# Cross network, last layer: the first half of the batch by features, the second half by rows

## The chip, the cores and the metric

The kernel runs on one NeuronCore of a Trainium2 chip. What is measured is the device time of one execution, in microseconds (us). A core has TensorE (PE: matrix multiplication into PSUM), VectorE (DVE: elementwise work), ScalarE (ACT: here it moves results out of PSUM and adds a bias), GpSimd (POOL: a few copies) and SyncE (SP: it issues DMAs, in order). The DMAs themselves are carried out by 16 DMA engines that the queues share. On-chip tiles lie in SBUF, which has 128 partitions.

## The reference

```python
B, F, D, L = 4096, 26, 16, 6          # Din = 416
def reference(x0, ws, bs):            # x0 (4096, 416), ws (6, 416, 416), bs (6, 416), all bf16
    x = x0
    for l in range(ws.shape[0]):
        x = x0 * (x @ ws[l] + bs[l]) + x
    return x
```

Six layers; each multiplies the batch by a 416 x 416 matrix, adds a bias, multiplies by the input and adds the layer's own input.

## The kernel before, in words

The 416 features are three blocks of 128 (`NK`, main) and a remainder of 32 (`R`). The batch of 4096 is two halves of 2048 (`s`), each of four groups of 512 columns (`g`).

*Layers 0 to 4 go by features.* The activations are transposed: `XM[i]` holds features on partitions (three blocks) and the batch along the row, `XR[i]` the remainder's 32 features, the four groups stacked on partitions. For a half `s` and a block `m`, `mm_full` (lines 201 to 207) gives 12 matmuls of 128x512 for each group, each of 32 output columns, so that four run side by side; `mm_row` (209) adds the remainder's part; `mm_rem` (215) computes the remainder's outputs. Results lie in PSUM, which is handed out two banks at a time, four such pairs in turn (`two_banks`, 142). `ew_main` (172) then takes 1024 columns: ScalarE moves them to a tile `t` with the bias (line 169), VectorE multiplies by x0 (line 179) and adds the layer's input (line 180). `ew_rem` (191) does the same for the remainder, 512 columns. Of `t` there are six buffers.

*The last layer (l = 5) goes by rows.* Its output has to lie in DRAM with the batch along rows. Therefore activations are the stationary operand there: a quad `q` (eight of them, four for each half) is 4 x 128 rows of the batch; each 128 rows by 416 outputs take three matmuls (`mm_q_full`, line 357) and one for the remainder (366) and one for the bias (371). ScalarE copies the result out of PSUM (383), VectorE multiplies by `X0rows` (384) and adds `XLrows` (385), SP stores rows of 832 B (387, 389). The last two quads do this for 128 rows at a time (`ew_single`, lines 396 to 401), with the sum put off until the next product has been issued.

For that, the last layer needs x0 and its own input by rows. `X0rows` is loaded from DRAM by eight DMAs (128). `XLrows` comes from layer 4: as soon as a half and block is done there, a transposing DMA (`xl_dmat`, line 229) turns it from SBUF to SBUF; the remainder's 32 features go through a transposing DMA into `scrR` (299) and a copy on POOL (300).

*What sets the order.* The schedule is manual: each engine does its instructions in the order in which the program writes them, and waits on semaphores where an operand isn't there. SP issues all stores and transposes of this stage in one order on one hardware queue (`q1`).

Of the kernel before, what the change touches and what calls it, by code (L numbers as in the profile page):

```python
# [10 lines left out]
ALU = mybir.AluOpType  # L11
BF16 = mybir.dt.bfloat16
# [4 lines left out]
def kernel(  # L17
# [7 lines left out]
    nc = tc.nc  # L25
    B, D = x0.shape
    L = ws.shape[0]
    P = 128
    NK = 3
    R = D - NK * P  # L30
    assert R == 32 and B == 4096 and D == 416 and L >= 2
    NS = 2
    NG = 4
    CW = 512
    SW = NG * CW
    NBT = B // P
# [20 lines left out]
    bT = const.tile([R, D // R, R], BF16)  # L57
    bM = const.tile([P, NK, L], FP32)
    bR = const.tile([P, L], FP32)
    X0rows = big.tile([P, NBT, D], BF16)  # L60
    XLrows = big.tile([P, NBT, D], BF16)
    scrR = [big.tile([P, 4, P], BF16, name=f"scrR{s}") for s in range(NS)]
    xrt = [big.tile([P, 16, R], BF16, name=f"xrt{s}") for s in range(NS)]
    xrem = [big.tile([P, 16, R], BF16, name=f"xrem{s}") for s in range(NS)]
# [4 lines left out]
    def col0(s, g):  # L69
        return SW * s + CW * g  # L70
# [54 lines left out]
        load_wr(nc.sync, g, 1, L)  # L125
    for l in range(2, L):
        load_wm(nc.sync, l)
    for q in range(8):
        nc.sync.dma_start(X0rows[:, 4 * q:4 * q + 4, :], x0_v[:, 4 * q:4 * q + 4, :])

    def fill_wd(l0, l1):
        for g in range(NG):
# [9 lines left out]
    def two_banks():  # L142
        n = turn[0]
        i = first_order[n] if n < len(first_order) else (2, 1, 3, 0)[(n - len(first_order)) % 4]
        turn[0] += 1
        return PS[:, 2 * i:2 * i + 2, :]
# [25 lines left out]
    def ew_main(l, s, m, h, pt, cur, nxt):  # L172
        c0 = col0(s, 2 * h)
        t = ew_copy(l, m, pt)
        x0c = XM[0][:, m, c0:c0 + 2 * CW]
        if l == 0:
            nc.vector.tensor_tensor(out=nxt[:, m, c0:c0 + 2 * CW], in0=t, in1=x0c, op=ALU.mult)  # L177
            return
        nc.vector.tensor_tensor(out=t, in0=t, in1=x0c, op=ALU.mult)  # L179
        nc.vector.tensor_tensor(out=nxt[:, m, c0:c0 + 2 * CW], in0=t, in1=cur[:, m, c0:c0 + 2 * CW], op=ALU.add)  # L180
# [20 lines left out]
    def mm_full(l, s, m, g, pts, cur, first, last):  # L201
        c0 = col0(s, g)
        for k in range(NK):
            for q in range(4):
                nc.tensor.matmul(pts[g // 2][32 * q:32 * q + 32, g % 2, :], lhsT=WM[:, l, k, 128 * m + 32 * q:128 * m + 32 * q + 32],  # L205
                                 rhs=cur[:, k, c0:c0 + CW], start=(first and k == 0), stop=(last and k == NK - 1),
                                 tile_position=(0, 32 * q), skip_group_check=True)
# [17 lines left out]
    def new_pts():  # L225
        return [two_banks() for h in range(2)]

    def xl_dmat(s, k, nxt):
        nc.sync.dma_start_transpose(out=XLrows[:, 16 * s:16 * s + 16, 128 * k:128 * k + 128],
                                    in_=nxt[:, k, SW * s:SW * s + SW])  # L230

# [58 lines left out]
    def rem_pair(l, cur, curR, nxtR, feeds_last):  # L292
        pr2 = two_banks()
        for s in range(NS):
            mm_rem(l, s, pr2[:, s, :], cur, curR)
        for s in range(NS):
            ew_rem(l, s, pr2[:, s, :], curR, nxtR)
            if feeds_last:
                nc.sync.dma_start_transpose(out=scrR[s][:], in_=nxtR[:, CW * s:CW * s + CW])
                nc.gpsimd.tensor_copy(XLrows[:, 16 * s:16 * s + 16, NK * P:D].rearrange("p (g i) r -> p i g r", g=NG),  # L300
                                      scrR[s][:].rearrange("p i (g r) -> p i g r", g=NG))

    def rem_first(pb):
        pr2 = two_banks()
# [10 lines left out]
    for l in range(1, LL):  # L315
        nxt, nxtR = XM[1 + (l % 2)], XR[1 + (l % 2)]
        feeds_last = (l == LL - 1)
        tiles = [(s, m) for s in range(NS) for m in range(NK)]
        pts = {}

        def finish(t):
            s, m = t
            for h in range(2):
                ew_main(l, s, m, h, pts[t][h], cur, nxt)
            if feeds_last:
                xl_dmat(s, m, nxt)

        for n in range(0, len(tiles), 2):
            ta, tb = tiles[n], tiles[n + 1]
            pts[ta] = new_pts()  # L330
            for g in range(NG):
                mm_full(l, ta[0], ta[1], g, pts[ta], cur, True, False)
            mm_row(l, ta[0], ta[1], pts[ta], curR, False, True)
            pts[tb] = new_pts()
            mm_row(l, tb[0], tb[1], pts[tb], curR, True, False)
            finish(ta)
            for g in range(NG):
                mm_full(l, tb[0], tb[1], g, pts[tb], cur, False, True)
            finish(tb)
            if n == 0:  # L340
                rem_pair(l, cur, curR, nxtR, feeds_last)
        cur, curR = nxt, nxtR

    l = LL
    quads = [(s, i) for s in range(NS) for i in range(4)]
    NQ = len(quads)
    KD = NK * P

    def q_cols(q, g):
        s, i = quads[q]  # L350
        c = col0(s, g) + 128 * i
        return slice(c, c + 128)

    def mm_q_full(q, py, gs, first):
        for g in gs:
            for k in range(NK):
                nc.tensor.matmul(py[g // 2][:, g % 2, 0:D], lhsT=cur[:, k, q_cols(q, g)], rhs=WM[:, l, k, :],  # L357
                                 start=(first and k == 0), stop=((not first) and k == NK - 1), skip_group_check=True)
# [2 lines left out]

    def mm_q_rows(qs, pys, begun):
        for q, py in zip(qs, pys):
            s, i = quads[q]
            for g in range(NG):
                nc.tensor.matmul(py[g // 2][:, g % 2, 0:D], lhsT=curR[32 * g:32 * g + 32, CW * s + 128 * i:CW * s + 128 * i + 128],
                                 rhs=WR[32 * g:32 * g + 32, l, :], start=not (q == begun and g < 2), stop=False,
                                 tile_position=(32 * g, 0), skip_group_check=True)
        for q, py in zip(qs, pys):
            for g in range(NG):  # L370
                nc.tensor.matmul(py[g // 2][:, g % 2, 0:D], lhsT=pick[1][32 * g:32 * g + 32, :],
                                 rhs=bsb[32 * g:32 * g + 32, :], start=False, stop=(q == begun and g < 2), tile_position=(32 * g, 0),
                                 skip_group_check=True)

    o4 = [big.tile([P, NG, D], BF16, name=f"o4_{q}") for q in range(3)]

    def ew_pair(q, h, py):
        s, i = quads[q]
        b0 = 16 * s + 8 * h + i
        t = tpool.tile([P, 2 * CW], BF16, name="t")  # L380
        tv = t[:, 0:2 * D].rearrange("p (a d) -> p a d", a=2)
        o = o4[q][:, 2 * h:2 * h + 2, :] if q < 3 else opool.tile([P, 2, D], BF16, name="o")[:]
        nc.scalar.copy(tv, py[h][:, :, 0:D])  # L383
        nc.vector.tensor_tensor(out=tv, in0=tv, in1=X0rows[:, b0:b0 + 5:4, :], op=ALU.mult)  # L384
        nc.vector.tensor_tensor(out=o, in0=tv, in1=XLrows[:, b0:b0 + 5:4, :], op=ALU.add)  # L385
        if q >= 3:
            nc.sync.dma_start(out_v[:, b0:b0 + 5:4, :], o)
        elif h == 1:
            nc.sync.dma_start(out_v[:, b0 - 8:b0 + 5:4, :], o4[q][:])

    def ew_single(q, g, py):
        s, i = quads[q]
        b = 16 * s + 4 * g + i
        t = tpool.tile([P, 2 * CW], BF16, name="t")
        o = opool.tile([P, 2, D], BF16, name="o")
        nc.scalar.copy(t[:, 0:D], py[g // 2][:, g % 2, 0:D])  # L396
        nc.vector.tensor_tensor(out=t[:, 0:D], in0=t[:, 0:D], in1=X0rows[:, b, :], op=ALU.mult)  # L397

        def close():
            nc.vector.tensor_tensor(out=o[:, 0, :], in0=t[:, 0:D], in1=XLrows[:, b, :], op=ALU.add)  # L400
            nc.sync.dma_start(out_v[:, b, :], o[:, 0, :])

        return close

    for q in range(0, NQ - 2, 2):
        py = [new_pts()]
        mm_q_full(q, py[0], (0, 1), True)
        py.append(new_pts())
        mm_q_rows((q, q + 1), py, q)
        ew_pair(q, 0, py[0])  # L410
        mm_q_full(q, py[0], (2, 3), False)
        ew_pair(q, 1, py[0])
        for h in range(2):
            mm_q_full(q + 1, py[1], (2 * h, 2 * h + 1), False)
            ew_pair(q + 1, h, py[1])
    pending = []
    for q in range(NQ - 2, NQ):
        py = new_pts()
        mm_q_rows((q,), (py,), None)
        for g in range(NG):  # L420
            mm_q_full(q, py, (g,), False)
            pending.append(ew_single(q, g, py))
            keep = 0 if (q, g) in ((NQ - 2, NG - 1), (NQ - 1, 0), (NQ - 1, NG - 1)) else 1
            while len(pending) > keep:
                pending.pop(0)()


# [28 lines left out]
```

## Time and profile before

| | |
|---|---|
| median of 3 timed runs | 130.84 us (130.61 to 131.32) |
| the profiled execution | 130.19 us, its span 128.13 us |
| granted TensorE clock | 1.00 |
| PE busy / VectorE busy / ScalarE busy | 122.7 / 105.2 / 83.5 us |
| layer 5 on PE | from 102.79 to 123.77 us |
| layer 5 on VectorE | from 106.94 to 125.39 us |
| landing of the last store | 127.3 us |

A line of a group or of the order of time names engine, line, operation, `out<-in`, and partitions x elements; `x6` is a count. "PE busy" counts matmuls in flight, so 96% doesn't say that PE is at its peak. An issue on SP is written SPq; "DMA to landing" is the time from the issue to the last write's confirmation. In a DMA view a queue's line has packets, MB, and the packets' time as a share of 16 engines; a share over 100% means that packets overlap.

### The profile page before, as it was taken

To read this page: it belongs to the slowest core of one execution; us is meant where nothing else is said; L and a number is where in the kernel's file an instruction comes from. 1 tells how busy PE (TensorE), PEld (TensorE's weight loads), DVE (VectorE), ACT (ScalarE), POOL (GpSimd) and SP (SyncE) were. 2 spreads that over 40 slices of the span, in tenths; PEclk is the share of its full clock that TensorE was granted. 3 is DMA by queue.
4 is the path that set the end of the run, shared out by engine and by line. 5 is a ranking of instruction groups with operands and counts; after the bars stand their busy time and mean duration, and the time that the engine had idled before them with its cause. 6 is when DMAs were issued, how large, how long until landed. Compare 5 with 4: busy or idle time off the path is not lost. (4 is left out here: it accounts for less than half of the span.)

```text
span 128.1 us, 3929 instructions
## 1 busy us (share of the span) xinstructions
PE 122.7 (96%) x1677; PEld 54.7 (43%) x1677; DVE 105.2 (82%) x192; ACT 83.5 (65%) x94; POOL 8.6 (7%) x29
## 2 busy tenths in 40 slices
PE   6999999999999999999999999999999999999960
PEld 3344344444444444444444544444444445445420
DVE  3347959357979898989898989898989999999991
ACT  2117559489666849666849666749666777567860
POOL 4282000120000000000000000000000300000000
PEclk9999999999999999999999999999999999999999
DMA  3999999999990000000000000000398899986663
GB/s 91 259 157 192 207 187 263 229 329 332 336 314 24 5 0 8 0 0 5 0 5 0 5 0 5 0 0 5 69 140 177 167 122 246 192 283 216 210 225 103
DMA packets 42029, 16.36 MB, mean 128 GB/s; under 512 B 30838, under 2 KB 42012, under 8 KB 42012
## 3 DMA queue, kind: packets, MB, share of 16 engines
q1 hardware_dynamic: 40512, 15.70, 55.0%
q10 hardware_dynamic: 1500, 0.42, 1.6%
q8 instruction: 13, 0.21, 0.7%
q14 instruction: 4, 0.03, 0.1%
HBM read 6.15 MB, written 3.41 MB: 75 GB/s over the span
## 5 line engine op out<-in xcount | busy, mean ns | idle before, releaser
L169 ACT ACTIVATE t<-PS,bM 128x1024 bf16<-128x1024 f32 x56 | 58.1, 1115 | 21.2 <-PE PS L211 21.2
L205 PE MATMUL PS<-XM,WM 128*32 128x512 bf16 x1152 | 65.2, 379 | 0.0
L205 PEld LDWEIGHTS <-WM 128*32 128x32 bf16 x1152 | 29.8, 97 | 33.7 <-issue 5.1
L179 DVE TENSOR_TENSOR t<-t,XM 128x1024 bf16<-128x1024 bf16 x48 | 33.4, 695 | 4.1 <-ACT t L169 4.1
L180 DVE TENSOR_TENSOR XM<-t,XM 128x1024 bf16<-128x1024 bf16 x48 | 33.5, 699 | 3.1
L357 PE MATMUL PS<-WM,XM 128*128 128x416 bf16 x96 | 17.9, 340 | 0.0
L240 PE MATMUL PS<-XM,WM 128*128 128x512 bf16 x72 | 16.5, 383 | 0.1
L383 ACT CAST t<-PS 128x832 bf16<-128x832 f32 x12 | 10.2, 852 | 5.0 <-PE PS L357 2.5
L357 PEld LDWEIGHTS <-XM 128*128 128x128 bf16 x96 | 8.9, 98 | 8.7 <-issue 2.1
L240 PEld LDWEIGHTS <-WM 128*128 128x128 bf16 x72 | 6.9, 99 | 9.4 <-issue 2.1
L222 PE MATMUL PS<-XM,WM 128*32 128x512 bf16 x120 | 8.2, 379 | 0.0
L193 ACT ACTIVATE t<-PS,bR 128x512 bf16<-128x512 f32 x10 | 6.8, 694 | 1.9 <-POOL WD L133 1.9
L385 DVE TENSOR_TENSOR o<-t,XLrows 128x832 bf16<-128x832 bf16 x12 | 7.1, 592 | 0.5
L211 PE MATMUL PS<-XR,WR 32*128 32x512 bf16 x96 | 7.3, 379 | 0.0
L384 DVE TENSOR_TENSOR t<-t,X0rows 128x832 bf16<-128x832 bf16 x12 | 7.0, 586 | 0.0
L300 POOL COPY XLrows<-scrR 128x512 bf16<-128x512 bf16 x2 | 1.4, 698 | 72.7 <-DMA scrR<-XR 72.7
L177 DVE TENSOR_TENSOR XM<-t,XM 128x1024 bf16<-128x1024 bf16 x7 | 4.7, 690 | 1.5 <-ACT t L169 1.4
L150 PE MATMUL PS<-warm 128*128 128x512 bf16 (+2 forms) x13 | 4.6, 536 | 1.0 <-DVE warm L87 1.0
L186 ACT ACTIVATE t<-PS,bM 128x512 bf16<-128x512 f32 x4 | 2.6, 685 | 3.8 <-PE PS L247 3.8
L162 ACT COPY XR<-xrt 64x256 bf16<-64x256 bf16 x2 | 1.2, 621 | 5.7 <-DVE xrt L161 5.7
L161 DVE STREAM_TRANSPOSE xrt<-xrem 64x256 bf16<-64x256 bf16 (+1 forms) x5 | 2.2, 477 | 3.2 <-DMA xrem<-in_x_dram 3.2
L396 ACT CAST t<-PS 128x416 bf16<-128x416 f32 x8 | 4.0, 506 | 1.0 <-PE PS L357 0.8
(44 smaller groups left out, 54.4 us busy)
## 6 DMA issues: line engine op xcount, KB each, us to landing
X0rows<-in_x_dram SPq DMA_DIRECT2D x8, 416.0 KB, 7.5
WM<-in_ws_dram SPq DMA_DIRECT2D x5, 312.0 KB, 6.7
out_dram<-o SPq DMA_DIRECT2D x3, 416.0 KB, 3.2
out_dram<-o SPq DMA_DIRECT2D x6, 208.0 KB, 2.5
out_dram<-o SPq DMA_DIRECT2D x8, 104.0 KB, 1.7
WR<-in_ws_dram SPq DMA_DIRECT2D x4, 130.0 KB, 5.7
WM<-in_ws_dram ACTq DMA_DIRECT2D x1, 312.0 KB, 3.4
XM<-in_x_dram SPq DMA_TRANSPOSE x8, 4.8
```

The source lines that it names most:

```text
L169: nc.scalar.activation(t[:], pt.rearrange("p a b -> p (a b)"), ACT.Identity, bias=bM[:, m, l:l + 1], scale=1.0)
L179: nc.vector.tensor_tensor(out=t, in0=t, in1=x0c, op=ALU.mult)
L180: nc.vector.tensor_tensor(out=nxt[:, m, c0:c0 + 2 * CW], in0=t, in1=cur[:, m, c0:c0 + 2 * CW], op=ALU.add)
L193: nc.scalar.activation(tr[:, 0:CW], pr, ACT.Identity, bias=bR[:, l:l + 1], scale=1.0)
L205: nc.tensor.matmul(pts[g // 2][32 * q:32 * q + 32, g % 2, :], lhsT=WM[:, l, k, 128 * m + 32 * q:128 * m + 32 * q + 32], rhs=cur[:, k, c0:c ...
L211: nc.tensor.matmul(pts[g // 2][:, g % 2, :], lhsT=WR[32 * g:32 * g + 32, l, 128 * m:128 * m + 128], rhs=curR[32 * g:32 * g + 32, CW * s:CW ...
L222: nc.tensor.matmul(pr[32 * g:32 * g + 32, :], lhsT=WM[:, l, k, NK * P:D], rhs=cur[:, k, c0:c0 + CW], start=False, stop=(k == NK - 1), tile ...
L240: nc.tensor.matmul(pt[:, gl, :], lhsT=WM[:, 0, k, 128 * m:128 * m + 128], rhs=cur[:, k, c0:c0 + CW], start=(first and k == 0), stop=(last ...
L357: nc.tensor.matmul(py[g // 2][:, g % 2, 0:D], lhsT=cur[:, k, q_cols(q, g)], rhs=WM[:, l, k, :], start=(first and k == 0), stop=((not first ...
L383: nc.scalar.copy(tv, py[h][:, :, 0:D])
L384: nc.vector.tensor_tensor(out=tv, in0=tv, in1=X0rows[:, b0:b0 + 5:4, :], op=ALU.mult)
L385: nc.vector.tensor_tensor(out=o, in0=tv, in1=XLrows[:, b0:b0 + 5:4, :], op=ALU.add)
```

## The change

The last layer does its two halves in two ways. The first half (s = 0) goes by features as the layers before it: `full_first` and `row_first` for the matmuls, `ew_main` and `ew_rem` for the rest, into `XM` and `XR`. Its result goes to rows by transposing DMAs into a new tile `Orows` (`to_rows`, and `rem_to_rows` for the remainder through `scrR` and POOL), and from there to DRAM by three stores of 128, 128 and 160 columns (`store_first`: 2048 pieces of 256, 256 and 320 B). So the first half needs neither `X0rows` nor `XLrows`: these tiles are halved, `X0rows` is loaded by one DMA, and layer 4's three transposes and the remainder's for the first half go. The second half stays by rows, as four quads: quad 0 in pairs of 128-row groups, quad 1's first two as a pair, the other ten alone. The order of VectorE's products (step 0) and sums (step 1) of these eleven units is written out in `order`. The output tiles `o4` go; all row stores use `o`, of which there are ten buffers. `mm_q_rows` now issues a quad's remainder and bias matmuls together.

```diff
+    HB = NBT // NS
+    X0rows = big.tile([P, HB, D], BF16)
+    XLrows = big.tile([P, HB, D], BF16)
+    Orows = big.tile([P, HB, D], BF16)
...
-    for q in range(8):
-        nc.sync.dma_start(X0rows[:, 4 * q:4 * q + 4, :], x0_v[:, 4 * q:4 * q + 4, :])
+    nc.sync.dma_start(X0rows[:], x0_v[:, HB:NBT])
...
+    def to_rows(rows, s, k, x):
+        nc.sync.dma_start_transpose(out=rows[:, :, 128 * k:128 * k + 128], in_=x[:, k, SW * s:SW * s + SW])
+
+    def rem_to_rows(rows, s, xR):
+        nc.sync.dma_start_transpose(out=scrR[s][:], in_=xR[:, CW * s:CW * s + CW])
+        nc.gpsimd.tensor_copy(rows[:, :, NK * P:D].rearrange("p (g i) r -> p i g r", g=NG),
+                              scrR[s][:].rearrange("p i (g r) -> p i g r", g=NG))
...
+        if feeds_last:
+            rem_to_rows(XLrows, 1, nxtR)
...
-            if feeds_last:
-                xl_dmat(s, m, nxt)
+            if feeds_last and s == 1:
+                to_rows(XLrows, 1, m, nxt)
...
+    def ew_rows(q, g0, g1, py):
+        b, n = 4 * g0 + q, g1 - g0
+        t = tpool.tile([P, 2 * CW], BF16, name="t")
+        tv = t[:, 0:n * D].rearrange("p (a d) -> p a d", a=n)
         o = opool.tile([P, 2, D], BF16, name="o")
+        nc.scalar.copy(tv, py[g0 // 2][:, g0 % 2:g0 % 2 + n, 0:D])
+
+        def product():
+            nc.vector.tensor_tensor(out=tv, in0=tv, in1=X0rows[:, b:b + 4 * n - 3:4, :], op=ALU.mult)
+
+        def total():
+            nc.vector.tensor_tensor(out=o[:, 0:n, :], in0=tv, in1=XLrows[:, b:b + 4 * n - 3:4, :], op=ALU.add)
+            nc.sync.dma_start(out_v[:, HB + b:HB + b + 4 * n - 3:4, :], o[:, 0:n, :])
+
+        return product, total
+
+    def store_first(d0, d1):
+        nc.sync.dma_start(out_v[:, 0:HB, d0:d1], Orows[:, :, d0:d1])
...
+    opened = [[False] * NG for m in range(NK)]
+    pt0 = new_pts()
+    full_first(0, pt0, 0)
+    row_first(0, pt0, (0, 1))
+    pt1 = new_pts()
+    row_first(1, pt1, ())
+    ew_main(l, 0, 0, 0, pt0[0], cur, nxt)
+    full_first(0, pt0, 1)
+    to_rows(Orows, 0, 0, nxt)
+    store_first(0, P)
+    for h in range(2):
+        full_first(1, pt1, h)
+    to_rows(Orows, 0, 1, nxt)
+    pr = two_banks()
+    mm_rem(l, 0, pr[:, 0, :], cur, curR)
+    ew_rem(l, 0, pr[:, 0, :], curR, nxtR)
+    rem_to_rows(Orows, 0, nxtR)
+    store_first(P, 2 * P)
+    pt2 = new_pts()
+    full_first(2, pt2, 0)
+    row_first(2, pt2, (0, 1))
+    py = [new_pts()]
+    mm_q_rows((0,), py, None)
+    ew_main(l, 0, 2, 0, pt2[0], cur, nxt)
+    full_first(2, pt2, 1)
+    to_rows(Orows, 0, 2, nxt)
+    for h in range(2):
+        mm_q_full(0, py[0], (2 * h, 2 * h + 1), False)
+        for step in ew_rows(0, 2 * h, 2 * h + 2, py[0]):
+            step()
...
+    order = [(0, 0), (1, 0), (0, 1), (1, 1), (2, 0), (3, 0), (2, 1), (3, 1), (4, 0), (5, 0), (4, 1), (6, 0), (5, 1), (6, 1),
+             (7, 0), (8, 0), (7, 1), (9, 0), (8, 1), (10, 0), (9, 1), (10, 1)]
+    units = []
+
+    def evict(q, g0, g1, pyq):
+        units.append(ew_rows(q, g0, g1, pyq))
+        while order and order[0][0] < len(units):
+            u, step = order.pop(0)
+            units[u][step]()
+            if (u, step) == (3, 1):
+                store_first(2 * P, D)
```

More of the change, by code (lines that the diff above doesn't have):

```diff
@@ L59 @@
     bR = const.tile([P, L], FP32)
-    X0rows = big.tile([P, NBT, D], BF16)
-    XLrows = big.tile([P, NBT, D], BF16)
+    HB = NBT // NS
+    X0rows = big.tile([P, HB, D], BF16)
+    XLrows = big.tile([P, HB, D], BF16)
+    Orows = big.tile([P, HB, D], BF16)
     scrR = [big.tile([P, 4, P], BF16, name=f"scrR{s}") for s in range(NS)]
@@ L226, in new_pts @@
         return [two_banks() for h in range(2)]
-    def xl_dmat(s, k, nxt):
-        nc.sync.dma_start_transpose(out=XLrows[:, 16 * s:16 * s + 16, 128 * k:128 * k + 128],
-                                    in_=nxt[:, k, SW * s:SW * s + SW])
+    def to_rows(rows, s, k, x):
[4 more added lines that the diff above has]
+                              scrR[s][:].rearrange("p i (g r) -> p i g r", g=NG))
     def first_layer(s):
@@ L297, in rem_pair @@
             ew_rem(l, s, pr2[:, s, :], curR, nxtR)
-            if feeds_last:
-                nc.sync.dma_start_transpose(out=scrR[s][:], in_=nxtR[:, CW * s:CW * s + CW])
-                nc.gpsimd.tensor_copy(XLrows[:, 16 * s:16 * s + 16, NK * P:D].rearrange("p (g i) r -> p i g r", g=NG),
-                                      scrR[s][:].rearrange("p i (g r) -> p i g r", g=NG))
+        if feeds_last:
+            rem_to_rows(XLrows, 1, nxtR)
     def rem_first(pb):
@@ L324, in finish @@
                 ew_main(l, s, m, h, pts[t][h], cur, nxt)
-            if feeds_last:
-                xl_dmat(s, m, nxt)
+            if feeds_last and s == 1:
+                to_rows(XLrows, 1, m, nxt)
         for n in range(0, len(tiles), 2):
@@ L344 @@
     l = LL
-    quads = [(s, i) for s in range(NS) for i in range(4)]
-    NQ = len(quads)
+    nxt, nxtR = XM[1 + (l % 2)], XR[1 + (l % 2)]
+    NQ = 4
     KD = NK * P
     def q_cols(q, g):
-        s, i = quads[q]
-        c = col0(s, g) + 128 * i
+        c = col0(1, g) + 128 * q
         return slice(c, c + 128)
@@ L363, in mm_q_rows @@
         for q, py in zip(qs, pys):
-            s, i = quads[q]
             for g in range(NG):
-                nc.tensor.matmul(py[g // 2][:, g % 2, 0:D], lhsT=curR[32 * g:32 * g + 32, CW * s + 128 * i:CW * s + 128 * i + 128],
+                nc.tensor.matmul(py[g // 2][:, g % 2, 0:D], lhsT=curR[32 * g:32 * g + 32, CW + 128 * q:CW + 128 * q + 128],
                                  rhs=WR[32 * g:32 * g + 32, l, :], start=not (q == begun and g < 2), stop=False,
                                  tile_position=(32 * g, 0), skip_group_check=True)
-        for q, py in zip(qs, pys):
             for g in range(NG):
@@ L373, in mm_q_rows @@
                                  skip_group_check=True)
[L375 to L379, printed above, removed]
+    def ew_rows(q, g0, g1, py):
+        b, n = 4 * g0 + q, g1 - g0
         t = tpool.tile([P, 2 * CW], BF16, name="t")
[L381 to L394, printed above, removed]
-        o = opool.tile([P, 2, D], BF16, name="o")
[L396 to L419, printed above, removed]
-        for g in range(NG):
[L421 to L425, printed above, removed]
+        tv = t[:, 0:n * D].rearrange("p (a d) -> p a d", a=n)
@@ new lines, in full_first, with row_first @@
+    def full_first(m, pt, h):
+        for g in (2 * h, 2 * h + 1):
+            mm_full(l, 0, m, g, pt, cur, not opened[m][g], opened[m][g])
+        if opened[m][2 * h]:
+            ew_main(l, 0, m, h, pt[h], cur, nxt)
+    def row_first(m, pt, begun):
+        for g in range(NG):
+            nc.tensor.matmul(pt[g // 2][:, g % 2, :], lhsT=WR[32 * g:32 * g + 32, l, 128 * m:128 * m + 128],
+                             rhs=curR[32 * g:32 * g + 32, 0:CW], start=(g not in begun), stop=(g in begun),
+                             tile_position=(32 * g, 0), skip_group_check=True)
+            opened[m][g] = True
@@ new lines @@
+    units = []
[6 more added lines that the diff above has]
+                store_first(2 * P, D)
+    py = [new_pts()]
+    mm_q_full(1, py[0], (0, 1), True)
+    py.append(new_pts())
+    mm_q_rows((1, 2), py, 1)
+    evict(1, 0, 2, py[0])
+    for q in (1, 2, 3):
+        if q == 3:
+            py.append(new_pts())
+            mm_q_rows((3,), (py[2],), None)
+        for g in range(2 if q == 1 else 0, NG):
+            mm_q_full(q, py[q - 1], (g,), False)
+            evict(q, g, g + 1, py[q - 1])
```

## The prediction

> **What bounds the kernel now.** I read the page first (busy shares, the span in slices, the chain that ended last), then the last stage in order of time, engine by engine, and then what the DMA queue and SP do there.
>
> The page, shares of the span, the span in 40 slices and the chain:
>
> ```profile
> PE 122.7 (96%) x1677; PEld 54.7 (43%) x1677; DVE 105.2 (82%) x192; ACT 83.5 (65%) x94; POOL 8.6 (7%) x29
> ...
> DVE  3347959357979898989898989898989999999991
> ...
> DMA  3999999999990000000000000000398899986663
> ...
> DVE 6%; issue 0%; DVEq 0%
> ```
>
> VectorE (DVE) is at 9 in the last ten slices, and the chain that ended last is VectorE alone. DMA is idle in the middle and works again only from slice 29 on. The last stage of VectorE in order of time (start, length):
>
> ```profile
> 99.35 1.10 DVE L179 TENSOR_TENSOR t<-t,XM 128x1024 bf16<-128x1024 bf16 x1
> 100.55 1.01 DVE L180 TENSOR_TENSOR XM<-t,XM 128x1024 bf16<-128x1024 bf16 x1
> 101.49 0.68 DVE L179 TENSOR_TENSOR t<-t,XM 128x1024 bf16<-128x1024 bf16 x1
> ...
> 106.33 0.69 DVE L180 TENSOR_TENSOR XM<-t,XM 128x1024 bf16<-128x1024 bf16 x1
> 106.94 0.58 DVE L384 TENSOR_TENSOR t<-t,X0rows 128x832 bf16<-128x832 bf16 x1
> 107.61 0.59 DVE L385 TENSOR_TENSOR o<-t,XLrows 128x832 bf16<-128x832 bf16 x1
> 108.12 0.58 DVE L384 TENSOR_TENSOR t<-t,X0rows 128x832 bf16<-128x832 bf16 x1
> ```
>
> VectorE enters the last layer at 106.94, while PE began it at 102.79. It then runs a product and a sum every 1.13 us until it has caught up with PE near the end: PE's last group starts at 121.49 and takes 2.28 (123.77), the last sum ends at 125.39, its store lands at 127.3. So both engines end together; neither alone can give much. Now SP and the DMAs, from the DMA view of a stretch of transposes, the source view of the transposes' line, and SP in order of time:
>
> ```profile
> q1 hardware_dynamic: 3080, 0.78, 125.2%
> ...
> XLrows<-XM SPq DMA_TRANSPOSE x2, 5.1
> ```
>
> ```profile
> L229 SPq DMA_TRANSPOSE XLrows<-XM x6: 1929/2722/3287, 90.6 to 107.4; - x6
> ...
> DMA to landing us min/median/max: 4.7/5.5/6.2
> ```
>
> ```profile
> 90.64 5.82 SPq L229 DMA_TRANSPOSE XLrows<-XM  x2
> 96.56 2.53 SPq L299 DMA_TRANSPOSE scrR<-XR  x2
> 99.18 11.33 SPq L229 DMA_TRANSPOSE XLrows<-XM  x4
> 110.60 3.64 SPq L389 DMA_DIRECT2D out_dram<-o  x3
> ```
>
> One transposing DMA of 128x2048 occupies SP for 1.9 to 3.3 us and lands 4.7 to 6.2 us after its issue. Today SP only issues: what it waits for is VectorE, never a landing, and the first store starts when the last transpose has been issued (110.60). The 3080 packets of 256 B in the first DMA view filled 125.2% of 3 us on 16 engines: 19.5 ns each.
>
> **The change part by part.** The profiled execution took 130.19 us, 2.06 more than its span of 128.13; its last store landed 0.85 before the span's end. The median of the timed runs is 130.84, 0.65 above it. I sum against the profiled execution and add the 0.65 at the end.
>
> *PE.* New: the first half's 144 column-split matmuls (six blocks of 24; 96 of them took 94.25 to 99.55, so 1.33 a block), 7.95; their row matmuls, 8 in 0.54 (99.55 to 100.09) and 4 in 0.27; the remainder's 16, 0.86 (89.29 to 90.15); four quads at 2.21 (118.81 to 121.02) and their row matmuls 0.47 + 0.81 + 0.47. Sum 20.2 against 102.79 to 123.77 = 21.0: 0.8 less. It does not reach the end, since VectorE is later.
>
> *VectorE.* In layer 4 one of POOL's two copies goes; the sums beside them took 1.10 and 1.01 instead of 0.69, some 0.37 a copy, and the layer before has an idle 0.29 at this place. VectorE therefore starts the last layer about 0.36 earlier, at 106.6. There: six pairs by features at 1.36 (four took 101.49 to 106.94), 8.2; remainder 0.87; the moved copy 0.37; quad 0's two pairs 2.26; then the fixed order, which puts no sum right behind its own product: 1.02 for the pair of 832 (0.51 from a sum to the next product) and 10 x 0.57. Sum 18.4, end at 125.0, 0.4 before today's 125.39. ACT has about 15 us of work there, beside 20 of PE.
>
> *The load of X0rows* is half as large and one issue instead of eight; the old ones had landed by 40, the first use is after 115: nothing. *Three transposes and a remainder's of the first half* leave SP and the queue between 90 and 105, where only VectorE's results were waited for: nothing either.
>
> *SP and the queue in the last layer* are what decides. SP works in order, and its new list is: transpose 0, store of columns 0 to 127, transpose 1, the remainder's transpose, store of columns 128 to 255, transpose 2, six row stores, store of columns 256 to 415, seven row stores. Each column store must wait on SP until its transpose has landed, and everything behind it waits too, later transposes with data long ready among them.
>
> Prices. A transpose: 4.7 to 6.2 to landing; I take 5.1, the median in both undisturbed stretches of the DMA view. Its first packets move 1.2 after the issue (90.64 to about 91.85: the DMA share is 0.00 up to 91.5 and 0.27 in the half us after). A single row store lands after 1.7, its 128 packets take 0.31; I put 1.1 of the rest before them and 0.4 behind the last. A column store has 2048 packets of 256 or 320 B, and stores below 832 B do not occur in the trace. Bounds: the 256-byte transposing packets at their full 287 GB/s, 1.8 us for the store; the 832-byte stores' 38.4 ns a packet (71.3% of 12.9 us on 16 engines, 3831 packets), 4.9 us. By time per packet nearest is 19.5 ns at the same size: 2.5 us. For 320 B, between 19.5 and 38.4 by size, 21.8 ns: 2.8 us (ends 2.3 and 4.9). A 2048-packet issue takes SP 0.6 (xrem's).
>
> The sum. Transpose 0 issues when VectorE has made two pairs, 106.6 + 2.8 = 109.4, and lands at 114.5. Store 0 issues at 114.55, packets 115.65 to 118.15. Transpose 1 issues at 115.2 and alone would begin at 116.4; behind store 0 it begins 1.75 later and lands at 122.05. The remainder's transpose takes SP 1.2 meanwhile, hidden by that landing, and its POOL copy follows near 123. Store 1 issues at 122.1; transpose 2 at 122.75, shifted alike, lands at 129.6. The six row stores (1152 packets, 2.76 us) follow its packets, 129.1 to 131.9. Store 2 issues at 129.65, its packets run 131.9 to 134.7; the seven row stores (896 packets, 2.15 us) to 136.8, landed at 137.2. With 0.85 the span is 138.05, with 2.06 the execution 140.1, with 0.65 a median of **140.8**. VectorE's end moves too, unimportantly: thirteen output tiles share ten buffers, so the last three sums wait for the row stores at the head of that queue (landing 130.1 to 131.4), about 132 instead of 125.
>
> The traced 256-byte packets are transposes inside SBUF, 19.5 ns each. The Trainium skill (DMA: Bandwidth & Descriptors, Specifications) puts line rate at 512 bytes and more and says that shorter transfers are done as read-modify-write; by that rule 256 and 320 bytes to HBM cost well over the transposing row, and the time comes nearer to rival 1. No trace here shows it. The same page (Why small descriptors are slow) counts 11 bus cycles for a 256-byte descriptor, 3 of them overhead; against 29 for 832 bytes that is an estimate of 15 ns, or 1.9 us a store, and the sum would be 1 to 2 us lower.
>
> **The rivals.**
> 1. *Short stores cost as much per packet as the 832-byte ones.* For it: they are writes to HBM, the only such row. Against: all 256-byte rows are half as dear. x 4.9 twice and 4.9 once: 2.4 + 2.4 + 2.1 more, 147.7. The Trainium skill's rule named above is a reason of the same direction and has no price there.
> 2. *The queue overlaps better*: transposes land in 4.7, do not queue behind stores, stores at 287 GB/s. Landings at 114.1, 119.5, 124.9; SP is free for store 2 at 125.7; packets end at 131.65; 135.6. For it: 125.2% busy shows that packets overlap. Against: all of it is one queue, and in the before trace stores begin only when the transposes' packets end.
> 3. *Not slower: the columns' way out stays hidden* and VectorE decides, 130.4 (0.4 less); if PE decided, at best 124.4 for the last sum, 129.8. Store 2's packets would have to end by 125.8, so it must issue by 122.4; from 109.4, less two issues of 0.65, three transposes must land in 3.9 each. The quickest of six took 4.7.
> That PE's gain does not come at all would change nothing in the sum.
>
> **How the numbers follow.** Main sum 0.60; rival 1, 0.17; rival 2, 0.17; rival 3, 0.06, split between faster and same (0.5%, or 0.65 us, is about what can be told from no change). Range: from rival 2's 135.6 less its uncertainty, 135.0, to rival 1's 147.7, 148.0; outside are rival 3 and the slower transposes (6.2 each: 3.3 more) on top of rival 1. The main sum's own range is 137.7 to 144.1: quick transposes (4.7) and cheap stores (1.8, 2.3) take off 3.1, slow transposes (6.2) add 3.3.
>
> **What would show it.** In the profile after: transposes of line 231 followed by a long gap on SP that a DMA's landing ends, three times; line 396's three stores, about 7.5 us from one to the next; VectorE's last three sums waiting for out_dram; PE's last matmul near 123; the DMA row at 9 well past 125. I am wrong if SP's waits for landings are short, if PE or VectorE is busy to the end, or if the column stores' packets take under 15 or over 35 ns.

## The result, and the profile after

The changed kernel takes 141.94 us (median of 6 runs, 141.36 to 143.75), the kernel before 130.79 us (6 runs beside them). The ratio is 1.0834, with a 95% interval of 1.0797 to 1.0872: slower by 8%. It is worked out from the single runs without the slowest (143.75), which fell in a slower state, so it is not the quotient of the two medians. The forecast was 140.8, in a range of 135.0 to 148.0.

The page of the kernel after, shares and span in 40 slices:

```profile
PE 121.6 (87%) x1767; PEld 53.9 (39%) x1769; DVE 104.9 (75%) x192; ACT 84.0 (60%) x94; POOL 8.5 (6%) x29
...
DVE  2358679259898989898898989898999999950300
...
DMA  4999999998000000000000000002069996969994
...
DMA 7%; SPq 4%; issue 0%; DVE 0%; DVEq 0%
```

PE and VectorE have as much to do as before, a little less even. But VectorE falls to almost nothing in the last eighth, while the DMA row goes on at 9 to the end, and the chain that ended last, VectorE alone before, is now DMA and SP. SP in order of time shows why (start, length, count):

```profile
101.99 8.75 SPq L231 DMA_TRANSPOSE XLrows<-XM  x3
110.84 3.46 SPq L231 DMA_TRANSPOSE Orows<-XM  x1
115.72 0.39 SPq L396 DMA_DIRECT2D out_dram<-Orows  x1
116.21 4.30 SPq L231 DMA_TRANSPOSE Orows<-XM  x1
120.61 1.22 SPq L234 DMA_TRANSPOSE scrR<-XR  x1
123.94 0.38 SPq L396 DMA_DIRECT2D out_dram<-Orows  x1
124.42 4.38 SPq L231 DMA_TRANSPOSE Orows<-XM  x1
128.89 3.12 SPq L391 DMA_DIRECT2D out_dram<-o  x6
132.12 0.39 SPq L396 DMA_DIRECT2D out_dram<-Orows  x1
132.56 5.16 SPq L391 DMA_DIRECT2D out_dram<-o  x7
```

Line 396 is a column store, line 391 a row store, line 234 the remainder's transpose. The gap ahead of the first (114.30 to 115.72) and of the second (121.83 to 123.94) is SP waiting for a transpose's landing; transpose 1 stands behind the first gap, transpose 2 behind both, though VectorE had its data ready at 116.5, eight us before its issue at 124.42. The third landing is hidden by the six row stores, which had been ready since 117.7 and issue only at 128.89. VectorE in order of time shows the other end of this:

```profile
123.98 0.37 DVE L387 TENSOR_TENSOR t<-t,X0rows 128x416 bf16<-128x416 bf16 x1
131.27 0.38 DVE L390 TENSOR_TENSOR o<-t,XLrows 128x416 bf16<-128x416 bf16 x1 [6.92 <-DMA out_dram<-o]
131.56 0.37 DVE L387 TENSOR_TENSOR t<-t,X0rows 128x416 bf16<-128x416 bf16 x1
...
132.55 0.38 DVE L390 TENSOR_TENSOR o<-t,XLrows 128x416 bf16<-128x416 bf16 x1 [0.25 <-DMA out_dram<-o]
```

VectorE stands for 6.92 us, until a row store frees an output buffer. Last, the DMA views of two column stores, 125.0 to 127.0 (256-byte pieces; from about 126.6 on transpose 2's packets are among them) and 133.2 to 135.7 (320-byte pieces); a queue's line has packets, MB, share of 16 engines:

```profile
q1 hardware_dynamic: 1635, 0.42, 94.1%
...
q1 hardware_dynamic: 1890, 0.60, 97.2%
```

That is 94.1% of 2 us x 16 / 1635 = 18.4 ns a packet of 256 B, and 20.6 ns a packet of 320 B (97.2% of 2.5 us). How fast the queue gets through them is another figure, since packets can overlap: from 125.0 to 126.5 it carries 1286 packets, so 2048 of 256 B take 2.4 us (219 GB/s), and 2048 of 320 B take 2.7 us (242 GB/s).

### The profile page after: what moved, and what is told of

Read it like the earlier page. It is cut to its first block, busy times and chain, and to the rows that moved or that the text cites. A ratio compares the mean times of both kernels' runs of the same rounds, so it can differ in the third digit from the quotient of the medians.

```text
span 139.9 us, 4097 instructions
## 1 busy us (share of the span) xinstructions
PE 121.6 (87%) x1767; PEld 53.9 (39%) x1769; DVE 104.9 (75%) x192; ACT 84.0 (60%) x94; POOL 8.5 (6%) x29
## 5 line engine op out<-in xcount | busy, mean ns | idle before, releaser
L171 ACT ACTIVATE t<-PS,bM 128x1024 bf16<-128x1024 f32 x62 | 64.8, 1114 | 24.0 <-PE PS L213 21.3
L207 PE MATMUL PS<-XM,WM 128*32 128x512 bf16 x1296 | 73.5, 379 | 0.0
L207 PEld LDWEIGHTS <-WM 128*32 128x32 bf16 x1296 | 33.4, 97 | 37.9 <-issue 5.8
L181 DVE TENSOR_TENSOR t<-t,XM 128x1024 bf16<-128x1024 bf16 x54 | 37.5, 694 | 4.1 <-ACT t L171 4.1
L182 DVE TENSOR_TENSOR XM<-t,XM 128x1024 bf16<-128x1024 bf16 x54 | 37.4, 692 | 3.6
L390 DVE TENSOR_TENSOR o<-t,XLrows 128x416 bf16<-128x416 bf16 (+1 forms) x13 | 5.2, 420 | 7.3 <-DMA out_dram<-o 7.2
L224 PE MATMUL PS<-XM,WM 128*32 128x512 bf16 x132 | 9.0, 379 | 0.0
L362 PE MATMUL PS<-WM,XM 128*128 128x416 bf16 x48 | 9.0, 340 | 0.0
L384 ACT CAST t<-PS 128x416 bf16<-128x416 f32 (+1 forms) x13 | 7.6, 585 | 1.8 <-PE PS L362 0.8
L362 PEld LDWEIGHTS <-XM 128*128 128x128 bf16 x48 | 4.5, 98 | 4.4 <-issue 0.7
L179 DVE TENSOR_TENSOR XM<-t,XM 128x1024 bf16<-128x1024 bf16 x7 | 4.7, 689 | 1.3 <-ACT t L171 1.1
L387 DVE TENSOR_TENSOR t<-t,X0rows 128x416 bf16<-128x416 bf16 (+1 forms) x13 | 5.1, 417 | 0.0
L224 PEld LDWEIGHTS <-WM 128*32 128x32 bf16 x132 | 3.5, 97 | 3.5
```

The source lines that it names most:

```text
L171: nc.scalar.activation(t[:], pt.rearrange("p a b -> p (a b)"), ACT.Identity, bias=bM[:, m, l:l + 1], scale=1.0)
L224: nc.tensor.matmul(pr[32 * g:32 * g + 32, :], lhsT=WM[:, l, k, NK * P:D], rhs=cur[:, k, c0:c0 + CW], start=False, stop=(k == NK - 1), tile ...
L384: nc.scalar.copy(tv, py[g0 // 2][:, g0 % 2:g0 % 2 + n, 0:D])
L387: nc.vector.tensor_tensor(out=tv, in0=tv, in1=X0rows[:, b:b + 4 * n - 3:4, :], op=ALU.mult)
L390: nc.vector.tensor_tensor(out=o[:, 0:n, :], in0=tv, in1=XLrows[:, b:b + 4 * n - 3:4, :], op=ALU.add)
```

## The experiments

The theory was: the output path of the first half costs by two things together, SP's waits for landings, which delay what stands behind them, and the packets themselves, which the 16 DMA engines must carry in the last 25 us. Rivals: waits alone; packets alone; short pieces dear by themselves; VectorE's wait for buffers. All ratios below are to the kernel before, run beside each experiment (130.41 us beside the stores put off, no column stores, no transposes and thirteen buffers; 130.53 beside the other four).

### Column stores put off

```diff
     to_rows(Orows, 0, 0, nxt)
-    store_first(0, P)
...
     rem_to_rows(Orows, 0, nxtR)
-    store_first(P, 2 * P)
+    store_first(0, P)
...
     to_rows(Orows, 0, 2, nxt)
+    store_first(P, 2 * P)
```

> The changed kernel, with the column stores later on SP: transposes 0 and 1 and the remainder's are issued one after the other, store 0 stands before transpose 2 and store 1 behind it. No store is moved far; only SP's waits for landings go. Theory (waits and packets together): in the profile of the changed kernel's times, transpose 1 issues near 114.3 instead of 116.2, transpose 2 near 119.2 instead of 124.4, and from there the queue is full: packets of store 0 to 122.3, of transpose 2 to 124.7, of store 1 to 127.1, six row stores to 129.9, store 2 to 132.6, seven row stores to 134.8. Last landing 135.1 instead of 139.1, time about 138. Rival W (SP's waits are all of it): with them gone the end is VectorE's again, 130 to 132. Rival P (the packets alone, the waits cost nothing): no change, 141 to 142.

Measured: 138.05 us, ratio 1.0590 (1.0554 to 1.0627). SP in order of time:

```profile
109.42 5.25 SPq L231 DMA_TRANSPOSE Orows<-XM  x2
114.76 1.80 SPq L234 DMA_TRANSPOSE scrR<-XR  x1
116.66 0.53 SPq L396 DMA_DIRECT2D out_dram<-Orows  x1
117.28 4.84 SPq L231 DMA_TRANSPOSE Orows<-XM  x1
...
128.29 5.22 SPq L391 DMA_DIRECT2D out_dram<-o  x7
```

Transpose 2 issues at 117.28 instead of 124.42, yet the time falls by 2.4% of the kernel before, 3.2 us, only. From then on the queue is most of the bound. Over the stretch from 119.5 to 134.4 its DMA view has

```profile
q1 hardware_dynamic: 9082, 3.56, 98.6%
```

That share counts packets that stand waiting too, and has a hole in it: from 120.9 to 122.0 it is 84.3%, with only 130 packets and 30 GB/s. From 122.0 to 132.0 packets follow one another with hardly a hole (7108 of them, 267 GB/s). The last row stores then go at SP's pace, one issue every 0.49 us. The theory's 138 was met; rival W falls (the waits are not all), and rival P too (they are 3.2 us).

### No column stores, and no transposes, and neither

Without the column stores (the first half of the output is not written):

```diff
     def store_first(d0, d1):
-        nc.sync.dma_start(out_v[:, 0:HB, d0:d1], Orows[:, :, d0:d1])
+        return
```

> The changed kernel without its three column stores: the first half of the output is not written, the transposes that feed them stay. Theory: the transposes run one behind the other and end near 122.5, the row stores behind them (2.8 us for six) catch up with VectorE, and the last sum, near 125.5, sets the end: 130 to 131, where the gain of PE and VectorE in the last layer would show (0.3 to 0.4 under the kernel before). Rival (the transposes alone are too much for SP and the queue): over 133.

Measured: 131.71 us, ratio 1.0101 (1.0063 to 1.0139). Below the rival's 133, but above the theory's 130 to 131, and above the kernel before, where a gain was expected.

Without the three main transposes (the calls of `to_rows` on `Orows` go, and POOL sets the tile to zero behind `fill_wd(1, L)`):

> The changed kernel without the three main transposes of the first half: its stores send zeros that POOL put into the tile early on; columns 0 to 383 of the first half are wrong by that, the stores are the same in number, size and place. Theory: the stores find their tile ready, issue as soon as SP reaches them (store 0 near 111), and 2.4 to 2.7 us each are hidden under VectorE's work: 130 to 131.5. Rival (the stores of 256 and 320 B are dear by themselves): 133 or more, with packets of 30 ns and more.

Measured: 132.01 us, ratio 1.0154 (1.0106 to 1.0202), half a us over the theory's range, under the rival's. Its column stores land 4.2 to 5.2 us after their issue, so they are not dear. So either one of the two is nearly hidden, and both together are not. To see what remained, I left out both:

```diff
-    to_rows(Orows, 0, 0, nxt)
...
-    to_rows(Orows, 0, 1, nxt)
...
-    rem_to_rows(Orows, 0, nxtR)
...
-    to_rows(Orows, 0, 2, nxt)
```

with `store_first` empty as above.

> The changed kernel without the first half's transposes, its remainder's POOL copy and its column stores: the first half of the output is not written; all work on PE, ScalarE and VectorE stays. Theory: this is what the change is worth on the engines: VectorE's last sum 0.2 to 0.4 before that of the kernel before, SP free to issue each row store at once, 130.0 to 130.4. The kernel without column stores alone was at 131.7, its last store issued 0.9 us after the last sum: SP, held by the transposes, was late, and that has to go here. Rival (VectorE or PE is slower in the new order): 131.5 again.

Measured: 130.07 us, ratio 0.9950 (0.9931 to 0.9970). This is what the change is worth on the engines, and it is a gain of 0.65 us (0.4 to 0.9 by the interval). SP in order of time, first of the kernel without column stores:

```profile
115.57 1.79 SPq L234 DMA_TRANSPOSE scrR<-XR  x1
117.45 1.93 SPq L231 DMA_TRANSPOSE Orows<-XM  x1
119.47 7.53 SPq L391 DMA_DIRECT2D out_dram<-o  x13
```

and then of the kernel without either:

```profile
117.79 8.37 SPq L391 DMA_DIRECT2D out_dram<-o  x13
```

The thirteen row stores begin 1.7 us later where SP has the transposes to issue, and run without a pause to 127.00 (the first takes 1.39, the last eight are 0.49 apart); the last sum had ended at 125.66, and the last store issues 0.9 behind it. Without the transposes the last store issues at 125.77, 0.2 behind the last sum at 125.60. That lag goes with the transposes, as the expectation said it should.

### Thirteen output buffers

```diff
-    opool = ctx.enter_context(tc.tile_pool(name="opool", bufs=10))
+    opool = ctx.enter_context(tc.tile_pool(name="opool", bufs=13))
```

> The changed kernel with 13 output buffers instead of ten. Theory: VectorE's 6.9 us wait for a row store's landing goes and its last sum ends near 125.5, but the time stays, 141.5 to 142.5, since those sums' stores stand behind store 2 on SP anyway. Rival (the wait for output buffers is on the path): 1 to 6 us faster.

Measured: 140.90 us, ratio 1.0817 (1.0787 to 1.0846), against 1.0834 (1.0797 to 1.0872) with ten: not to be told apart. In microseconds it is just under the forecast of 141.5, on a chip whose kernel before was faster too. VectorE in order of time ends with

```profile
124.69 0.65 DVE L390 TENSOR_TENSOR o<-t,XLrows 128x416 bf16<-128x416 bf16 x2
```

so the 6.92 us wait, the longest of VectorE in the profile after, is gone, and no gain can be told: it stood beside the queue.

### Column stores from POOL

```diff
-        nc.sync.dma_start(out_v[:, 0:HB, d0:d1], Orows[:, :, d0:d1])
+        nc.gpsimd.dma_start(out_v[:, 0:HB, d0:d1], Orows[:, :, d0:d1])
```

> The changed kernel with its three column stores issued by POOL instead of SP: POOL waits for the transposes' landings, SP for nothing but VectorE, and the stores' packets come from another queue of the same 16 DMA engines. Theory (waits on SP, then the queue's packets): transpose 2 issues near 117.5, the packets from 112 on (transposes 7.7 us, column stores 7.5, row stores 4.9) end at 132 if nothing leaves holes; 135 to 138, no better than 135. Rival W (only SP's waits matter): 130 to 132. Rival G (POOL is slow to issue a DMA of 2048 pieces): 138 or more.

Measured: 139.23 us, ratio 1.0659 (1.0625 to 1.0693). SP waits for no landing any more, but this is rather dearer than putting the stores off on SP (the two intervals just touch). The source view of the stores' line, from issue to landing, and POOL in order of time:

```profile
L396 POOL DMA_DIRECT2D out_dram<-Orows x3: 1152/1157/1373, 115.3 to 125.8; - x3
...
DMA to landing us min/median/max: 6.5/8.3/8.6
```

```profile
115.34 1.37 POOL L396 DMA_DIRECT2D out_dram<-Orows  x1 [16.23 <-DMA Orows<-XM]
123.74 0.97 POOL L235 COPY Orows<-scrR 128x512 bf16<-128x512 bf16 x1 [7.02 <-DMA scrR<-XR]
124.66 2.30 POOL L396 DMA_DIRECT2D out_dram<-Orows  x2
```

So the waiting in order has moved to POOL. Transpose 1 had landed at 118.01, but its column store stands on POOL behind the remainder's copy, which waits 7.02 us for its own transpose, and issues at 124.66. Besides, a store lands 8.3 us after its issue (median) instead of the 4.3 from SP. Rival G's time came out right; its reason, a slow issue, is the small part: 1.2 to 1.4 us an issue against 0.4 on SP. How much of the rest is POOL's order and how much the two queues beside each other was not tried.

### One store of whole rows

```diff
-    store_first(0, P)
...
-    store_first(P, 2 * P)
...
-                store_first(2 * P, D)
+                store_first(0, D)
```

> The changed kernel with one store of whole rows (2048 pieces of 832 B) in the place of the third column store, and no other column store. Theory: SP waits for one landing only, transposes end near 122.7, six row stores to 125, the large store's packets (2048 x 39 ns / 16 = 5.0 us) to 130, seven row stores to 132.2: about 135.5 to 136, some 2.5 us under the kernel with all column stores put off, since the packets take 5.0 us instead of 7.5. Rival (pieces do not matter, the order of the queue does): 138.

Measured: 136.31 us, ratio 1.0441 (1.0412 to 1.0470), 1.9 us below the stores put off (1.0590). Expected were 2.0 to 2.5. In a stretch of 832-byte packets alone (125.7 to 130.0, share of 16 engines 110.7%, 1730 packets) one takes 44 ns, but they overlap: 1730 in 4.3 us are 40 ns each on 16 engines, so 2048 take 5.1 us, as expected, against 7.5 in pieces (2.4 twice and 2.7). Here the queue carries packets from 122.0 to 132.2 without a hole (never under 317 GB/s), and the kernel ends with it. This is the best form of the change I ran, and it loses 4.4%.

### The order of sums alone, on the kernel before

```diff
-        nc.vector.tensor_tensor(out=o, in0=tv, in1=XLrows[:, b0:b0 + 5:4, :], op=ALU.add)
+        def close():
+            nc.vector.tensor_tensor(out=o, in0=tv, in1=XLrows[:, b0:b0 + 5:4, :], op=ALU.add)
...
+        pending.append(close)
+        while len(pending) > 1:
+            pending.pop(0)()
```

> The kernel before, with one part of the change alone: in the six quads that go by pairs a sum comes after the next product, not right behind its own. Theory: VectorE needs 1.02 instead of 1.13 us a pair, 1.3 us in all, but in the kernel before ScalarE's last copy out of PSUM ends at 124.3 and PE's last matmul sets that; after it there is a product and a sum to do whatever the order. At most 0.3 us: 130.1, which the rounds can hardly tell from 130.4. Rival (VectorE alone bounds the end): 129.1.

Measured: 130.76 us, ratio 1.0022 (1.0004 to 1.0040): no gain (the interval allows at most a loss of 0.4%). VectorE is quicker in the middle and then waits for ScalarE, and ScalarE for PE; waits of the last layer:

```profile
ACT t L383 <- PE PS L357: 2.7, 9, 0.5
...
DVE t L384 <- ACT t L383: 1.3, 4, 0.6
```

The kernel before has no wait of VectorE for ScalarE on that line. A VectorE made quicker in this way gives nothing there: by these waits PE sets the end of the kernel before, and VectorE, busy to nine tenths, follows it.

## Why the prediction was right, step by step

*The engines.* PE was to take 20.2 us for the last layer instead of 21.0. By the order of time, from the start of layer 4's last 48 matmuls to the end of the last one it was 100.09 to 123.77, 23.7, and is 100.81 to 123.70, 22.9: 0.8 less, as forecast. VectorE was to end 0.4 earlier; measured from the start of layer 0's remainder matmuls (24.00 before, 24.83 in the kernel with neither transposes nor column stores) the last sum comes 101.39 and 100.77 later, 0.6 earlier; that kernel has no POOL copy in the last layer, which I had charged with 0.37. Where the engines alone decide (rival 3's condition), the time is 0.65 us lower, so a rival of 0.4 was right in its direction and about in size. But it put the gain down to VectorE and said that PE's 0.8 does not reach the end; the order of sums alone gained nothing on the kernel before, so PE's 0.8 is likely part of the 0.65. No run divides the two. (Of the two slow instructions beside POOL's copies that the prediction calls sums, the one of 1.10 is a product.)

*SP in order, and what stands behind each wait.* The list of issues and landings, forecast and measured: transpose 0 issued at 109.4, measured 110.84; store 0 at 114.55 and 115.72; transpose 1 at 115.2 and 116.21; store 1 at 122.1 and 123.94; transpose 2 at 122.75 and 124.42; store 2 at 129.65 and 132.12; last landing 137.2 and 139.06. The 1.4 us by which the first step was late come from two things: this execution reached layer 0's remainder matmuls 0.7 us later than the one before (24.73 against 24.00), and the transpose ahead held SP until 110.75, while VectorE had the data at 110.2. The steps after it come 1.0 to 1.9 us late, and store 2 comes 2.5 late. The forecast saw three gaps on SP that a landing ends; there are two, since SP was not free when the third landed.

*Prices.* A transpose to landing was put at 5.1, and 6.85 behind a store: 18.8 for the three. Measured: 4.87, 7.66 and 6.06, 18.6. That the sum fits is in part luck: of the two behind a store, one took 0.8 more than the 6.85 (its tail is told in the last section) and the other 0.8 less. The column stores' packets were put at 2.5 and 2.8 us for 2048 pieces, from the traced 256-byte transposes; at the queue's pace above it is 2.4 and 2.7. So the number was right, and rival 1 was wrong: a packet of 256 B to HBM takes half as long as one of 832 B. But the reading behind the number was not sound. The 19.5 ns is the time that a packet is under way, in a stretch where packets overlap (125.2%); the queue got through one every 15.6 ns on 16 engines there, and at its best moved 287 GB/s, 1.8 us for 2048. The column store's packets hardly overlap, at 219 GB/s. So pieces of 256 B to HBM were slower than transposing packets at their best, and about as fast as those behind a store (206 GB/s from 119.0 to 121.5 of the profile after). That a figure which counts overlapping time came out at the stores' price is luck in part. The Trainium skill's rule of read-modify-write below 512 bytes (DMA: Bandwidth & Descriptors, Specifications) agrees in its direction, since 256 and 320 B move 219 and 242 GB/s here and 832 B 327 (112 to 114 of the profile before); whether a read-modify-write is the cause, no run here shows. Its count of bus cycles (same page, Why small descriptors are slow) gave an estimate of 15 ns, below the measured 18.4. The whole-row store shows what pieces cost: 7.5 us in short ones, 5.1 in long ones, for the same bytes.

*The mis-sized term.* What the sum had too low is the store 2 step: I had let it issue at transpose 2's landing (129.65 by the forecast). In the trace transpose 2 landed at 130.47, but SP was at the row stores until 132.01 and took up store 2 at 132.12, since transpose 2 had held SP for 4.38 us where the transposes of before held it 1.9 to 3.3. The sum takes SP to be free by then, without saying so. It cost little, since the row stores' packets were still running until 133. The other short term is the last seven row stores: I gave their packets 2.15 us at the queue's rate, but from 135.36 on SP issues one every 0.49 us, and their packets run from about 135.8 to 138.5, 2.7 us.

*The gain that did not arrive.* Added up by the ratios, in percent of the kernel before: engines alone -0.5; transposes without column stores +1.5 above that, column stores without transposes +2.0, both, with SP's waits for landings mostly out, +6.4; the waits another +2.4. The two costs are more than their sum, as I read it because each alone nearly fits under VectorE's work, while together the last 25 us have more packets than the queue can carry. The whole-row store supports that the queue bounds most of the last step: with the waits out and 2.4 us less of packets it gains 1.9 us, and its packets run without a hole to the end. What remains beside the queue is SP's pace with the last single row stores.

## What to carry to other kernels

A result that leaves through a chain of DMAs (transpose, landing, store) needs its time after the last computation. Here transpose and store take 9 us from issue to landing, the engines' gain was 0.65 us, and the change was a loss. On an in-order queue write down, for every issue that waits for a landing, what stands behind it, and put those issues last; then count the packets of the closing stretch against the DMA engines' rate, since waits taken out only bring that bound forward. A long wait in a profile (6.92 us of VectorE here) is worth nothing until a run without it is faster.

## What I had not expected of the hardware

A transpose's issue holds SP longer when its packets stand behind a store's in the queue: 4.30, 4.38 and, with the stores put off, 4.84 us (and 5.63 beside a store from POOL), against 1.3 to 3.5 behind nothing or another transpose; the row stores behind it then wait too. The same 2048 pieces issued by POOL land 8.3 us after the issue (median of three, beside other packets), from SP 4.3.

The time that a packet is under way is not the queue's pace: 832-byte packets took 44 ns each with the one large store and 38.4 in the kernel before, yet on 16 engines the queue got through one every 40 ns in both (before: 803 packets from 112 to 114). And a transpose can end in a long tail: transpose 1 in the profile after lands 7.66 us after its issue, and from 122.6 to 123.6 only 49 packets move (9 GB/s), behind a 16 KB packet of the instruction queue that took 0.88 us at 121.8. The kernel with one store has such a tail, 39 packets from 120.0 to 121.2, behind a like packet at 119.6. No run was made without these packets, so the cause is not shown.
